# Attention and two feed-forward blocks on one core: all engines and the transfers keep the order of the source

## The chip, the cores and the metric

The kernel runs on one core of a Trainium2 chip. The core's engines run side by side, each through its own list of instructions in order: TensorE (PE in the profile, with its weight loads as PEld), VectorE (DVE), ScalarE (ACT), GpSimd (POOL), and SyncE (SP), which here issues all transfers. The transfers run on 16 DMA engines. An engine that comes to an instruction whose input isn't there waits, and what stands behind it on that engine waits too. The metric is the device time of one execution, in microseconds.

## The reference

4 batches of 12 heads of 448 x 64. The scores of all heads are mixed by a 12 x 12 matrix before the softmax, and the weights by another one after it. The output, as 1792 tokens of 768, goes through two feed-forward blocks.

```python
scores = scale * np.matmul(q, k.transpose(0, 1, 3, 2))
scores = np.einsum('bhij,hg->bgij', scores, w_pre)
scores = scores - np.max(scores, axis=-1, keepdims=True)
attn = np.exp(scores)
attn = attn / (np.sum(attn, axis=-1, keepdims=True) + 1e-09)
attn = np.einsum('bhij,hg->bgij', attn, w_post)
x = np.matmul(attn, v)              # then as (1792, 768)
x = (((x @ w1) * (x @ w2)) @ w3) @ w_out
h = x @ w_in
return np.maximum(0.01 * h, h) @ w_out2
```

## The kernel before

**Tiles.** Each batch has its 448 query rows in four chunks of 120, 120, 120 and 88. A chunk has blocks of 10 query rows (12 blocks, in the last chunk 9, of which the last has 8 rows), so a block is 10 rows x 12 heads = 120 partitions. There are 180 blocks in 16 chunks.

**Scores.** `qk` multiplies q and k for a pair of heads. q and k are split before into a high part (ACT, line 77) and the rest (DVE, line 80), by `q_split` (for a chunk, 0.8 and 0.9 us) and `k_split` (for pairs of heads), and three products of the parts are added. ACT copies the result from PSUM to a tile `s` (DVE half of it in the first two chunks), and each four heads go to a DRAM buffer `sdr`. `relayout` reads them back as 120 partitions of (row, head), two blocks at once, into `sr`.

**A block's work.** `premix` mixes the heads by one matmul with `kpre` into a PSUM bank `pm` (two banks); DVE takes the maximum `mx`, ACT the exponential `e` with its sums `sm`; POOL adds 1e-9 to `sm`, DVE takes the reciprocal `rc`, POOL scales `kpost` by it into `kr`. `postmix`, three blocks behind (LAG), multiplies `e` and `kr` into `po`, and DVE copies this into `ap`. When a chunk is complete, `av` multiplies `ap` with v in two halves, DVE copies the result `px` to `y`, and it goes to `scr`.

**Work in between.** Weights of the feed-forward blocks come as 64-bit words: 32 pieces of `w_out` and `w3` are turned into 32-bit ones during the attention: a load to `wr`, an absolute value on ACT (line 96), four steps on DVE (lines 97 to 104), a store. `fold` multiplies them together at the start of the feed-forward part; the load and split of its first operand `wo` (ACT and POOL, line 385) already runs among the last blocks.

**What sets the order.** In the loop over the blocks (n, with t the block's place in its chunk), each pass calls premix of block n, relayout of n + 6 (AHEAD), the qk of the chunk two further on (QAHEAD; two pairs of heads at t = 0, 2 and 4, in the short chunk at 0, 1 and 2), loads and splits, av where due, postmix of n - 3. PE keeps this order (`manual_schedule` with PE alone). For DVE, ACT, POOL and for SP's queue of transfers, a planner with a model of times chooses the order, and so decides how far ahead of its reader a load stands. `issue_after` only keeps some transfers behind a relayout. q of a chunk is loaded at t = 4, split at t = 0 of the next one, ahead of the first qk that reads it:

```python
if ci + QAHEAD < len(order):
    if t % gap == 0 and t // gap < 3:
        if t == 0:
            q_split(*order[ci + QAHEAD])
        for p in (2 * t // gap, 2 * t // gap + 1):
            qk(*order[ci + QAHEAD], p)
if t == 4 and ci + QAHEAD + 1 < len(order):
    q_load(*order[ci + QAHEAD + 1])
```

Of the kernel before, what the change touches and what calls it, by code (L numbers as in the profile page):

```python
# [23 lines left out]
def attention_moe_kernel(ctx: ExitStack, tc, qt, kt, vt, w_pre, w_post, w1, w2, w3t, w_out, w_in2, w_out2, out):  # L24
# [7 lines left out]
    nc = tc.nc  # L32
# [11 lines left out]
    AHEAD, QAHEAD, LAG, START = 6, 2, 3, 20  # L44
# [46 lines left out]
    def convert(pool, t, shape):  # L91

# [4 lines left out]
        nc.vector.tensor_scalar(out=cf, in0=cf, scalar1=F64_TINY, scalar2=F64_HUGE, op0=ALU.max, op1=ALU.min)  # L97
        nc.vector.tensor_scalar(
            out=c, in0=c, scalar1=0x07FFFFFF, scalar2=3, op0=ALU.bitwise_and, op1=ALU.logical_shift_left
        )  # L100
        nc.vector.scalar_tensor_tensor(
            out=c, in0=hi, scalar=0xC0000000, in1=c, op0=ALU.bitwise_and, op1=ALU.bitwise_or
        )
        nc.vector.scalar_tensor_tensor(  # L104
            out=c, in0=lo, scalar=29, in1=c, op0=ALU.logical_shift_right, op1=ALU.bitwise_or
        )
        return cf

    def attention():
        with ExitStack() as es:  # L110
# [8 lines left out]
            es.enter_context(tc.manual_schedule(engines={mybir.EngineType.PE}))  # L119
# [7 lines left out]
            def constants():  # L127
                for n, w in enumerate((w_pre, w_post)):
                    nc.sync.dma_start(out=wrep[:, n, :], in_=w.unsqueeze(0).to_broadcast([IB, H, H]))
                eye = ident[:R, :R].rearrange("p (i h) -> p i h", h=H)  # L130
# [13 lines left out]
            gate, kls, qls, raws = {}, {}, {}, []  # L144
            kst, vst, qst, st = {}, {}, {}, {}
            srt, ets, krs, apt = {}, {}, {}, {}

            def k_load(b, g):

                kls[b, g] = ld.tile([P, 2, S], F32, tag="kl", name="kl", bufs=3)  # L150
                gate["k"] = nc.sync.dma_start(out=kls[b, g], in_=kt[b, :, 2 * g:2 * g + 2, :])

            def k_split(b, g):
                t = kls.pop((b, g))
                for r in range(2):
                    kst[b, 2 * g + r] = kv.tile([P, 2, S], F32R, tag="ks", name="ks", bufs=NPAIR + 2)
                    split(kst[b, 2 * g + r], t[:, r, :])
# [17 lines left out]
            def qk(b, c, p):  # L175
# [17 lines left out]
                if r == HP - 1:  # L193
                    nc.sync.dma_start(out=sdr[b, c][:, 2 * g * HP:2 * (g + 1) * HP, :], in_=st[b, c][:m])

            def relayout(n):

                b, c, t = blocks[n]
                bl = chunks[c][2]
                o, nb = bl[t]  # L200
                if t % 2 == 0:
                    pair = wk.tile([IB * H, 2, S], F32, tag="sr", name="sr", bufs=4)
                    if t + 1 < len(bl) and bl[t + 1][1] == nb:
                        src = sdr[b, c][o:o + 2 * nb].rearrange("(g i) h j -> (i h) g j", g=2)
                        gate["sr"] = nc.sync.dma_start(out=pair[:nb * H], in_=src)
# [6 lines left out]
            def premix(n):  # L212
                b, c, t = blocks[n]
# [13 lines left out]
                )  # L227
                rc = wk.tile([IB * H, 1], F32, tag="rc", name="rc")
                nc.gpsimd.tensor_scalar(out=sm[:r], in0=sm[:r], scalar1=1e-9, scalar2=None, op0=ALU.add)
# [5 lines left out]
                ets[n], krs[n] = e, kr  # L235

            def postmix(n):
                b, c, t = blocks[n]
# [15 lines left out]
                nc.vector.tensor_copy(ap[:, :, :, o:o + nb], po[:, :, :, :nb])  # L254

            def av(b, c, g):
# [18 lines left out]
                if g == 1:  # L275
                    nc.sync.dma_start(out=scr[b][:, :, c0:c0 + ni], in_=y[:, :, :ni])
# [3 lines left out]
            def conv_load(src, dst, r, c0, n):  # L280
                words = src[r * P:(r + 1) * P, 2 * c0:2 * (c0 + n)].unsqueeze(1)
                raws.append((load_raw(ws, words, (1, n), 2), dst, r, c0, n))

            def conv_store():
                t, dst, r, c0, n = raws.pop(0)
                nc.sync.dma_start(out=dst[r * P:(r + 1) * P, c0:c0 + n], in_=convert(ws, t, (1, n))[:, 0, :])

            blocks = [
                (b, c, t) for b in range(B) for c in range(len(chunks)) for t in range(len(chunks[c][2]))
            ]  # L290
            order = [(b, c) for b in range(B) for c in range(len(chunks))]
            first = {}
            for n, (b, c, t) in enumerate(blocks):
                if t == 0:
                    first[b, c] = n
# [6 lines left out]
            for g in range(NPAIR // 2):  # L302
                k_load(0, g)
                if g == 0:
                    constants()
# [281 lines left out]
```

## Time and profile before

| | us |
|---|---|
| median of three runs | 1523.85 |
| lowest, highest | 1516.05, 1526.09 |
| the profiled execution | 1523.08 |
| its span, first to last instruction | 1521.0 |
| mean granted TensorE clock | 0.956 |
| PE busy | 1406.3 (92%) |
| DVE busy | 908.6 (60%) |
| ACT busy | 585.5 (38%) |
| POOL busy | 179.2 (12%) |
| first matmul of `fold` | at 621.84 |

Busy times are of the span. The granted clock is the share of full speed at which the chip lets TensorE run. A wait is written "engine, tile, line <- what it waited for". In the groups, "x176 | 111.0, 631" means 176 instructions, 111.0 us busy, 631 ns for one. In the timeline the columns are start, length (us), engine, line, operation, output and inputs, and in brackets the idle time ahead of it. The lines `L185` (qk), `L218` (premix), `L222` (mx), `L225` (e), `L247` (postmix), `L254` (ap), `L267` (av) carry the attention; L77 and L80 are the two halves of every split.

### The profile page before, as it was taken

How to read it: one execution, taken by the hardware profiler on the slowest of the kernel's cores; microseconds unless marked ns; L12 is line 12 of the kernel's file. 1: busy time of each engine (PE TensorE's matmuls, PEld its weight loads, DVE VectorE, ACT ScalarE, POOL GpSimd, SP SyncE). 2: the span in 40 equal slices, each digit the busy share in tenths (PEclk: the TensorE clock that was granted, in tenths of full speed). 3: DMA queues.
4: the chain of work that ended last, by engine and by line, in shares of the span. 5: the costliest groups of instructions: out<-in, count | busy, mean ns of one | idle time of the engine just before them, and what ended most of it. 6: DMA issues, size and time to landing. Idle time of an engine off the chain costs nothing.

```text
span 1521.0 us, 22114 instructions
## 1 busy us (share of the span) xinstructions
PE 1406.3 (92%) x8520; PEld 1211.5 (80%) x8520; DVE 908.6 (60%) x1580; ACT 585.5 (38%) x1117; POOL 179.2 (12%) x374
## 2 busy tenths in 40 slices
PE   4778888888789889999999999999999999999999
PEld 2556656666566657999999999999999999999998
DVE  3455556556656546546653596696866445866962
ACT  3443444344434443333332264253333323552430
POOL 0222222232223354000000000000000000000000
PEclk7899989898889889999999999999999999999999
DMA  7757687679777874554312243333733132432301
GB/s 233 208 163 193 191 241 213 179 212 256 220 204 224 239 218 125 155 184 130 106 54 90 86 146 104 104 125 94 225 99 103 55 99 96 149 101 97 130 24 73
DMA packets 140116, 226.23 MB, mean 149 GB/s; under 512 B 19244, under 2 KB 117548, under 8 KB 139564
## 3 DMA queue, kind: packets, MB, share of 16 engines
q1 hardware_dynamic: 140012, 224.83, 49.7%
q8 instruction: 67, 1.10, 0.3%
q14 instruction: 37, 0.30, 0.1%
HBM read 164.77 MB, written 60.03 MB: 148 GB/s over the span
## 4 chain that ended last, share of the span: by engine, by line
PE 74%; DMA 15%; ACT 3%; DVE 3%; SPq 2%; issue 2%; POOL 0%; POOLq 0%; ACTq 0%; DVEq 0%
PE pm L455 39%; PE po L522 15%; DMA ql<-in_q_dram 6%; PE pm L218 5%; PE po L247 5%; DMA wr<-in_moe_w_dram 4%; PE pw L393 4%; PE px L267 3%; DMA wr<-in_moe_w_out_dram 3%; PE pq L185 2%; ACT e L225 1%; ACT s L192 1%; DMA wof<-wof 1%; DVE ap L254 1%; DMA kl<-in_k_dram 1%
## 5 line engine op out<-in xcount | busy, mean ns | idle before, releaser
L455 PE MATMUL pm<-x,ws 128*128 128x448 f32 x2304 | 477.7, 368 | 0.0
L455 PEld LDWEIGHTS pm<-x,ws 128*128 128x128 f32 x2304 | 432.4, 188 | 43.3
L247 PEld LDWEIGHTS po<-kr,e 120*112 120x112 f32 (+1 forms) x1440 | 181.8, 189 | 87.8 <-issue 68.4
L522 PE MATMUL po<-ws,g 128*128 128x384 f32 x1344 | 234.3, 334 | 0.0
L522 PEld LDWEIGHTS po<-ws,g 128*128 128x128 f32 x1344 | 233.2, 188 | 0.3
L247 PE MATMUL po<-kr,e 120*112 120x120 f32 (+1 forms) x1440 | 196.2, 283 | 17.8 <-DVE ap L254 12.5
L218 PE MATMUL pm<-sr,kpre 120*120 120x448 f32 x360 | 181.8, 590 | 30.8 <-ACT e L225 27.9
L225 ACT ACTIVATE e<-pm,mx 120x448 f32<-120x448 f32 x180 | 113.5, 631 | 187.0 <-DVE mx L222 118.2
L96 ACT ACTIVATE wc<-wr 128x768 f32<-128x768 f32 (+2 forms) x128 | 105.8, 830 | 154.3 <-DVE ws L80 57.9
L80 DVE TENSOR_TENSOR ws<-wc,ws 128x768 fp32r<-128x768 f32 x96 | 91.5, 955 | 82.1 <-ACT ws L77 80.9
L97 DVE TENSOR_SCALAR wc<-wc 128x768 f32<-128x768 f32 (+2 forms) x128 | 66.1, 517 | 119.6 <-ACT wc L96 119.5
L254 DVE COPY ap<-po 112x480 f32<-112x480 f32 x180 | 117.1, 650 | 31.8 <-PE po L247 25.7
L267 PEld LDWEIGHTS px<-ap,vs 112*64 112x64 f32 x1536 | 90.4, 159 | 46.7 <-ACT s L192 40.3
L222 DVE TENSOR_REDUCE mx<-pm 120x1 f32<-120x448 f32 x180 | 111.7, 621 | 26.4 <-PE pm L218 19.2
L232 POOL TENSOR_SCALAR kr<-kpost,rc 120x120 f32<-120x120 f32 x180 | 116.0, 644 | 96.5 <-DVE rc L230 47.9
L77 ACT ACTIVATE ws<-wc 128x768 fp32r<-128x768 f32 x96 | 80.6, 842 | 118.3 <-PE po L522 73.9
L267 PE MATMUL px<-ap,vs 112*64 112x120 f32 (+1 forms) x1536 | 97.3, 293 | 28.2 <-ACT s L192 20.0
L455 PE MATMUL pm<-h,ws 128*128 128x448 f32 x576 | 119.4, 368 | 0.0
L185 PE MATMUL pq<-ks,qs 64*120 64x448 f32 (+1 forms) x576 | 87.2, 419 | 34.0 <-DVE y L274 12.5
L185 PEld LDWEIGHTS pq<-ks,qs 64*120 64x120 f32 (+1 forms) x576 | 54.9, 191 | 78.4 <-issue 22.2
L455 PEld LDWEIGHTS pm<-h,ws 128*128 128x128 f32 x576 | 108.1, 188 | 10.9
L104 DVE SCALAR_TENSOR_TENSOR wc<-wr,wc 128x768 uint32<-128x768 uint32 (+2 forms) x128 | 111.6, 872 | 1.4
(45 smaller groups left out, 1059.9 us busy)
## 6 DMA issues: line engine op xcount, KB each, us to landing
sr<-sdr SPq DMA_DIRECT2D x88, 420.0 KB
sdr<-s SPq DMA_DIRECT2D x36, 840.0 KB
wr<-in_moe_w_dram SPq DMA_DIRECT2D x32, 768.0 KB
wr<-in_moe_w_in_dram SPq DMA_DIRECT2D x32, 768.0 KB
wr<-in_moe_w_out_dram SPq DMA_DIRECT2D x32, 768.0 KB
wr<-in_moe_w_dram SPq DMA_DIRECT2D x16, 512.0 KB
sdr<-s SPq DMA_DIRECT2D x12, 616.0 KB
wr<-in_moe_w_out_dram SPq DMA_DIRECT2D x16, 384.0 KB
```

Source lines behind the costliest of these rows:

```text
L96: nc.scalar.activation(out=cf, in_=hi.bitcast(F32), func=ACTF.Abs)
L104: nc.vector.scalar_tensor_tensor(out=c, in0=lo, scalar=29, in1=c, op0=ALU.logical_shift_right, op1=ALU.bitwise_or)
L185: nc.tensor.matmul(pq[e][:m], qst[b, c][rows, p, x, :m], kst[b, p][rows, y, :], start=(j == 0), stop=(j == 2))
L218: nc.tensor.matmul(pm[:r], kpre[:r, :nb, :].rearrange("p i h -> p (i h)"), sr[:r], start=True, stop=True)
L222: nc.vector.tensor_reduce(out=mx[:r], in_=pm[:r], axis=AX.X, op=ALU.max, negate=True)
L225: nc.scalar.activation(out=e[:r], in_=pm[:r], func=ACTF.Exp, bias=mx[:r], scale=1.0, accum_out=sm[:r])
L232: nc.gpsimd.tensor_scalar(out=kr[:r], in0=kpost[:r], scalar1=rc[:r], scalar2=None, op0=ALU.mult)
L247: nc.tensor.matmul(po[:, jc, :, :nb], e[:r, jc * JP:(jc + 1) * JP], kr[:r, :, :nb], start=True, stop=True,)
L254: nc.vector.tensor_copy(ap[:, :, :, o:o + nb], po[:, :, :, :nb])
L267: nc.tensor.matmul(px[e * D:(e + 1) * D, p - p0, :ni], vst[b][:, jc, 2 * p + e, :], ap[:, jc, 2 * p + e, :ni], start=(jc == 0), stop=(jc = ...
L455: nc.tensor.matmul(dst, wt[:, a, kk, :], x[:, kk, c, n * S:(n + 1) * S], start=(kk == 0 and j == 0), stop=(kk == kn - 1 and j == 2),)
L522: nc.tensor.matmul(po, g[:, m, a, t * P:(t + 1) * P], wts[m][:, c, 0, cs], start=(m == 0 and j == 0), stop=(m == FQ - 1 and j == 2),)
```

## The change

- `manual_schedule()` now holds for all engines, so within the attention DVE, ACT, POOL and SP run in the order of the source as PE did. `issue_after` goes.
- The source is written as a pipeline of steps. Of block n's work, premix stands first, then the reciprocal and `kr` of block n - 1 (`weigh`), then `sums` of block n, the relayout, qk, av and postmix of n - 3, then loads and splits.
- qk runs at t = 0, 2, 6. q is loaded at t = 4 and split at t = 7, for the chunk after the one whose qk is running; a third q is loaded and split ahead of the loop. k is loaded at t = 1 to 3 of the second chunk of a batch and split one pair of heads at a time, at t = 7 to 11 and at t = 1 of the third.
- Stores of `s`, `y` and converted weights are put in a list and issued at the start of the next step (`flush`).
- The conversion is a generator: in a step that has qk or av (t = 0, 2, 3, 4, 6), from n = 14 on, two of its pieces are issued; three loads are ahead.
- In the other steps, ap of every odd n is copied by ACT and no longer by DVE: 50 of 180.
- At the start all of k is loaded before the small constants, and v after q of the third chunk.

```diff
-    AHEAD, QAHEAD, LAG, START = 6, 2, 3, 20
+    AHEAD, QAHEAD, LAG, START = 6, 2, 3, 14
...
-            es.enter_context(tc.manual_schedule(engines={mybir.EngineType.PE}))
+            es.enter_context(tc.manual_schedule())
...
-                    nc.sync.dma_start(out=sdr[b, c][:, 2 * g * HP:2 * (g + 1) * HP, :], in_=st[b, c][:m])
+                    stores.append((sdr[b, c][:, 2 * g * HP:2 * (g + 1) * HP, :], st[b, c][:m]))
+
+            def flush():
+
+                while stores:
+                    dst, t = stores.pop(0)
+                    nc.sync.dma_start(out=dst, in_=t)
...
-                nc.vector.tensor_copy(ap[:, :, :, o:o + nb], po[:, :, :, :nb])
+                copy(ap[:, :, :, o:o + nb], po[:, :, :, :nb])
...
+                for _ in range(3):
+                    load()
+                yield
+                while raws:
+                    t, dst, n = raws.pop(0)
+                    for cf in convert_steps(ws, t, (1, n)):
+                        yield
+                    stores.append((dst, cf[:, 0, :]))
+                    load()
...
+            QT, AT = (0, 2, 6), (LAG, LAG + 1)
+            filler = conversions()
...
+            q_load(0, 2)
+            v_prep(0)
             for p in range(NPAIR):
                 qk(0, 1, p)
-            with tc.issue_after(gate["sr"].ins):
-                v_prep(0)
-                q_load(0, 2)
+                flush()
+            q_split(0, 2)
             for n in range(NB + LAG):
+                flush()
+                plain = True
                 if n < NB:
-                    b, c, t = blocks[n]
+                    b, c, t, _ = blocks[n]
                     ci = order.index((b, c))
-                    gap = (len(chunks[c][2]) - AHEAD) // 3
+                    plain = t not in QT and t not in AT
                     premix(n)
+                if 0 < n <= NB:
+                    weigh(n - 1)
+                if n < NB:
+                    sums(n)
                     if n + AHEAD < NB:
                         relayout(n + AHEAD)
...
+                    if ci + QAHEAD < len(order) and t in QT:
+                        for r in range(HP):
+                            qk(*order[ci + QAHEAD], HP * QT.index(t) + r)
                 m = n - LAG
                 if m >= 0:
                     tt = blocks[m][2]
                     if tt < 2 and m > tt:
                         av(*blocks[m - tt - 1][:2], tt)
-                    postmix(m)
+                    postmix(m, nc.scalar.copy if plain and n % 2 else nc.vector.tensor_copy)
+                if n < NB:
+                    if t == 4 and ci + QAHEAD + 1 < len(order):
+                        q_load(*order[ci + QAHEAD + 1])
+                    if t == 7 and ci + QAHEAD + 1 < len(order):
+                        q_split(*order[ci + QAHEAD + 1])
...
+                        if c == NC - 3 and 1 <= t < 4:
+                            k_load(b + 1, t - 1)
+                        if c == NC - 3 and t >= 7:
+                            k_split(b + 1, t - 7)
+                        if c == NC - 2 and t == 1:
+                            k_split(b + 1, 5)
+                    if n >= START and not plain:
+                        for _ in range(2):
+                            next(filler, None)
```

How the order moves is seen at three places. The first is ACT before the change, where the last scores of the third batch's first chunk are made: the copies of a qk (`s`), the absolute value of a weight piece (`wc`), an exponential, the split of q, and the copies of the next qk.

```order
L192 ACTIVATE s<-pq 120x448 x4
L96 ACTIVATE wc<-wr 128x384
L225 ACTIVATE e,sm<-pm,mx 120x448
L77 ACTIVATE qs<-ql 128x6x120
L225 ACTIVATE e,sm<-pm,mx 120x448
L192 ACTIVATE s<-pq 120x448 x4
```

So three instructions stand between the absolute value and the copies of the next qk. The loads of this `wr` and this `ql` stand on SP, among a store of converted weights (`wof`), a store of scores (`sdr`), a relayout (`sr`) and a store of the output (`scr`):

```order
L286 DMA wof<-wc 128x384
L88 DMA wr<-in_moe_w_out_dram 128x768
L194 DMA sdr_0_65<-s 120x1792
L205 DMA sr<-sdr_2_63 120x2x448
L165 DMA ql<-in_q_dram 128x720
L194 DMA sdr_0_65<-s 120x1792
L276 DMA scr_74<-y 768x1x120
```

One store and one relayout lie between the two loads. With the change, the split of the same q stands on ACT in a plain step, behind the last qk of the chunk before it and ahead of a copy of `ap`:

```order
L200 ACTIVATE s<-pq 120x448 x4
L101 ACTIVATE wc<-wr 128x384
L239 ACTIVATE e,sm<-pm,mx 120x448
L77 ACTIVATE qs<-ql 128x6x120
L239 ACTIVATE e,sm<-pm,mx 120x448
L276 COPY ap<-po 112x48x10
```

It is followed by an exponential and the copy, no longer by the qk that reads it. On SP this q is loaded ahead of the last store of the chunk before it:

```order
L219 DMA sr<-sdr_2_63 120x2x448
L173 DMA ql<-in_q_dram 128x720
L208 DMA scr_74<-y 768x1x120
L219 DMA sr<-sdr_3_64 120x2x448
L88 DMA wr<-in_moe_w_dram 128x1024
L208 DMA sdr_0_65<-s 120x1792
L208 DMA wof<-wc 128x384
```

The load now stands two steps ahead of that last store, and three steps ahead of the split.

The second place is DVE and ACT in the plain steps of a batch's second chunk, where q and k are split. ACT now has, between the exponentials (`e`), the splits (`qs`, `ks`) and a copy of `ap`:

```order
L239 ACTIVATE e,sm<-pm,mx 120x448
L77 ACTIVATE qs<-ql 128x6x120
L77 ACTIVATE ks<-kl 128x448
L239 ACTIVATE e,sm<-pm,mx 120x448
L276 COPY ap<-po 112x48x10
L77 ACTIVATE ks<-kl 128x448
L239 ACTIVATE e,sm<-pm,mx 120x448
```

A split stands between any two exponentials. Before, ACT had the k splits in pairs, among the copies of `s`:

```order
L225 ACTIVATE e,sm<-pm,mx 120x448
L77 ACTIVATE ks<-kl 128x448
L192 ACTIVATE s<-pq 88x448
L77 ACTIVATE ks<-kl 128x448
L192 ACTIVATE s<-pq 88x448
L225 ACTIVATE e,sm<-pm,mx 120x448
```

There two splits stood between two exponentials, with copies that need PE's results; now the splits are spread over six steps, and on DVE the other half of each stands ahead of the next maximum.

The third place is SP's queue at the start. Before, with three relayouts first, then a store of scores, v and q of the third chunk:

```order
L205 DMA sr<-sdr_0_57 120x2x448 x3
L194 DMA sdr_1_58<-s 120x1792
L161 DMA vs<-in_v_dram 112x3072
L165 DMA ql<-in_q_dram 128x720
L205 DMA sr<-sdr_0_57 120x2x448
```

There v and a store go ahead of q. Now:

```order
L219 DMA sr<-sdr_0_57 120x2x448 x3
L173 DMA ql<-in_q_dram 128x720
L169 DMA vs<-in_v_dram 112x3072
L208 DMA sdr_1_58<-s 120x1792 x3
L219 DMA sr<-sdr_0_57 120x2x448
```

q has moved ahead of v and of the stores, which still follow v.

More of the change, by code (lines that the diff above doesn't have):

```diff
@@ L227, in premix, with sums, weigh @@
                 )
+                ets[n], sms[n] = e, sm
+            def sums(n):
+                sm = sms[n][:blocks[n][3]]
+                nc.gpsimd.tensor_scalar(out=sm, in0=sm, scalar1=1e-9, scalar2=None, op0=ALU.add)
+            def weigh(n):
+                r = blocks[n][3]
+                sm = sms.pop(n)
                 rc = wk.tile([IB * H, 1], F32, tag="rc", name="rc")
-                nc.gpsimd.tensor_scalar(out=sm[:r], in0=sm[:r], scalar1=1e-9, scalar2=None, op0=ALU.add)
                 nc.vector.reciprocal(out=rc[:r], in_=sm[:r])
@@ L275, in av, with conversions, load @@
                 if g == 1:
-                    nc.sync.dma_start(out=scr[b][:, :, c0:c0 + ni], in_=y[:, :, :ni])
+                    stores.append((scr[b][:, :, c0:c0 + ni], y[:, :, :ni]))
             ys = {}
[L280 to L286, printed above, removed]
+            def conversions():
+                units = [(w_out, wof, r, c0, DM // 2) for r in range(DF // P) for c0 in (0, DM // 2)]
+                units += [(w3t, w3f, r, c0, DF // 2) for r in range(DF // P) for c0 in (0, DF // 2)]
+                raws = []
+                def load():
+                    if units:
+                        w, dst, r, c0, n = units.pop(0)
+                        words = w[r * P:(r + 1) * P, 2 * c0:2 * (c0 + n)].unsqueeze(1)
+                        raws.append((load_raw(ws, words, (1, n), 3), dst[r * P:(r + 1) * P, c0:c0 + n], n))
+                for _ in range(3):
[7 more added lines that the diff above has]
+                    load()
@@ L288, in attention @@
             blocks = [
-                (b, c, t) for b in range(B) for c in range(len(chunks)) for t in range(len(chunks[c][2]))
+                (b, c, t, chunks[c][2][t][1] * H)
+                for b in range(B) for c in range(len(chunks)) for t in range(len(chunks[c][2]))
             ]
             order = [(b, c) for b in range(B) for c in range(len(chunks))]
[L292 to L295, printed above, removed]
@@ L296, in attention @@
             NB = len(blocks)
-            units = [(w_out, wof, r, c0, DM // 2) for r in range(DF // P) for c0 in (0, DM // 2)]
-            units += [(w3t, w3f, r, c0, DF // 2) for r in range(DF // P) for c0 in (0, DF // 2)]
-            every = (NB - 8 - START) // len(units)
+            NC = len(chunks)
+            QT, AT = (0, 2, 6), (LAG, LAG + 1)
+            filler = conversions()
             q_load(0, 0)
@@ L316, in attention @@
             q_split(0, 1)
+            constants()
+            for n in range(AHEAD):
+                relayout(n)
+            q_load(0, 2)
+            v_prep(0)
             for p in range(NPAIR):
                 qk(0, 1, p)
-            with tc.issue_after(gate["sr"].ins):
-                v_prep(0)
-                q_load(0, 2)
+                flush()
+            q_split(0, 2)
             for n in range(NB + LAG):
+                flush()
+                plain = True
                 if n < NB:
-                    b, c, t = blocks[n]
+                    b, c, t, _ = blocks[n]
```

77 lines of the change are left out of this document (33 added, 44 removed).

## The prediction

> **What bounds the kernel now.** I read the stretches first, cut where the trace shows a new stage, because the page's shares are means over an attention part and a feed-forward part with different limits. The last row is the feed-forward part, from the first matmul of `fold` to the end.
>
> ```profile
> span 1521.0 us, 22114 instructions
> ...
> 26.17:60.16 33.99, 16.38 (x74) 8.94 (x75) 6.71 (x15) 10.45 (x24) 4.07 (x10) 0.70 0.81 244
> 60.16:551.00 490.84, 415.94 (x3202) 303.76 (x3203) 284.79 (x631) 209.39 (x516) 138.40 (x297) 0.90 0.75 210
> 551.00:576.00 25.00, 18.92 (x95) 12.16 (x95) 10.76 (x24) 11.72 (x24) 20.07 (x22) 0.80 0.89 236
> 576.00:621.84 45.84, 44.67 (x479) 35.88 (x473) 29.12 (x63) 15.88 (x39) 15.97 (x39) 1.00 0.35 92
> 621.84:1521.00 899.16, 895.29 (x4610) 840.12 (x4608) 564.34 (x825) 326.08 (x493) 0.00 (x0) 1.00 0.35 110
> ```
>
> The columns are the stretch, its length, the busy time of PE, PEld, DVE, ACT and POOL, the granted clock, the DMA share and GB/s. From 621.84 us on, PE is busy 895.29 of 899.16 us at full clock, and the change doesn't touch that code: it stays. The main loop of the attention, 60.16 to 551, is different. PE is busy 415.94 of 490.84 us at a granted clock of 0.90, so the work in it is 415.94 x 0.90 = 374.3 us of a full-clock PE, and 116.5 us are lost: 74.9 to idleness and 41.6 to the halved clock that follows idleness. No other engine is near its limit (DVE 284.79, DMA 0.75). So the loop is bound by waits, and the next views are the waits (engine, what it waited for, us, times, longest) and one of them in order of time.
>
> ```profile
> ACT qs L77 <- DMA ql<-in_q_dram: 51.9, 13, 9.0
> ACT wc L96 <- DMA wr<-in_moe_w_dram: 44.2, 14, 8.3
> ACT wc L96 <- DMA wr<-in_moe_w_out_dram: 35.0, 14, 5.4
> ...
> PE pm L218 <- ACT e L225: 27.9, 18, 4.3
> ...
> 274.42 2.41 SPq L88 DMA_DIRECT2D wr<-in_moe_w_out_dram  x1
> 277.90 1.96 SPq L165 DMA_DIRECT2D ql<-in_q_dram  x1
> 281.78 0.54 ACT L96 ACTIVATE wc<-wr 128x384 f32<-128x384 f32 x1 [5.40 <-DMA wr<-in_moe_w_out_dram]
> 286.65 0.80 ACT L77 ACTIVATE qs<-ql 128x720 fp32r<-128x720 f32 x1 [3.72 <-DMA ql<-in_q_dram]
> ...
> 284.00:288.00 4.00, 1.47 (x5) 0.79 (x5) 2.60 (x5) 1.35 (x4) 0.37 (x1) 0.50 0.28 71
> ```
>
> This is the whole story of the loop. SP issues the load of a weight piece at 274.42 and of the next q at 277.90; ACT stands at the instruction that reads it until 281.78 and 286.65, 7.4 and 8.75 us after the issues, because the order gives a transfer less time than it takes. Behind the waiting instruction on ACT stand the exponentials, behind them the two pm banks, and so PE: it is busy 1.47 us of the four, at half clock. 51.9 + 44.2 + 35.0 = 131.1 us of such waits in 41 places fit the 116.5 us lost.
>
> **The change, part by part.** First the lengths of the steps at full clock, from the starts of one premix and the next: a plain step, one with two qk pairs, one with an av.
>
> ```profile
> 297.80 0.92 PE L218 MATMUL pm<-sr,kpre 120*120 120x448 f32 x2
> 299.38 0.92 PE L218 MATMUL pm<-sr,kpre 120*120 120x448 f32 x2
> ...
> 272.24 0.92 PE L218 MATMUL pm<-sr,kpre 120*120 120x448 f32 x2
> 275.41 0.92 PE L218 MATMUL pm<-sr,kpre 120*120 120x448 f32 x2
> ...
> 603.15 0.92 PE L218 MATMUL pm<-sr,kpre 120*120 120x448 f32 x2
> 607.52 0.92 PE L218 MATMUL pm<-sr,kpre 120*120 120x448 f32 x2
> ...
> 448.00:496.00 48.00, 44.17 (x336) 31.12 (x334) 31.71 (x70) 22.48 (x56) 16.70 (x34) 1.00 0.81 230
> ```
>
> That is 1.58, 3.17 and 4.37 us.
>
> *Loads ahead of their readers.* q is now loaded at t = 4 and split at t = 7: an av step, a plain one and a qk step lie between (4.37 + 1.58 + 3.17), and the exponential of step 7, so some 10 us against the 8.75 us measured. The weight pieces are loaded three units ahead, a unit takes two of the five steps that are not plain, so over 15 us. Both waits should go. What the DMAs need: 0.75 x 490.84 = 368 us of all 16 engines for this stretch. At the share of 0.89 that the row of 551 shows this takes 413 us, so PE's 374.3 can't be reached, but 413 is a floor below what follows. I leave 6 us for q that comes late (0 where the lead holds, 13 x 3 = 39 where every q is 3 us late).
>
> *What the order of the source costs.* Now DVE and ACT run strictly as written, and the splits are written behind the step's exponential and ahead of the next maximum. The durations:
>
> ```profile
> L225 ACT ACTIVATE e<-pm,mx 120x448 f32<-120x448 f32 x176 | 111.0, 631 | 182.3 <-DVE mx L222 118.2 <-DVE rc L230 61.2 <-POOL sm L229 2.6
> L222 DVE TENSOR_REDUCE mx<-pm 120x1 f32<-120x448 f32 x176 | 109.2, 620 | 25.5 <-PE pm L218 18.6 <-ACT s L192 0.2
> L254 DVE COPY ap<-po 112x480 f32<-112x480 f32 x176 | 114.9, 653 | 30.9 <-PE po L247 24.8
> L192 ACT ACTIVATE s<-pq 120x448 f32<-120x448 f32 x120 | 56.8, 544 | 6.3 <-PE pq L185 6.1
> L77 ACT ACTIVATE qs<-ql 128x720 fp32r<-128x720 f32 x10 | 8.0, 801 | 42.1 <-DMA ql<-in_q_dram 42.1
> L80 DVE TENSOR_TENSOR qs<-ql,qs 128x720 fp32r<-128x720 f32 x10 | 9.0, 905 | 26.1 <-ACT qs L77 26.1
> L77 ACT ACTIVATE ks<-kl 128x448 fp32r<-128x448 f32 x18 | 9.5, 569 | 11.3 <-DMA kl<-in_k_dram 11.3
> L80 DVE TENSOR_TENSOR ks<-kl,ks 128x448 fp32r<-128x448 f32 x18 | 11.0, 624 | 12.0 <-ACT ks L77 12.0
> ```
>
> A q split at t = 7 makes a chain from one maximum to the next: mx 0.62, e 0.63, qs high 0.80, qs low 0.91, in all 2.96 us where a plain step has 1.58; where ACT also copies an ap, 0.54 more. PE waits for an exponential two steps back and so absorbs some 0.7 us, but the qk step ahead leaves DVE about 1 us late (its ap copy waits for po behind the qk, then come two conversion pieces). I take 2.05 us for the nine splits in a chunk of 12 blocks, 0.5 us for the others, whose next step is a qk step: about 20 us. A k split makes 0.62 + 0.63 + 0.57 + 0.62 = 2.44 us, with an ap copy on ACT 2.98; against 1.58 that is 1.13 over on the mean. It stands in t = 7 to 11 of the second chunk and t = 1 of the third, together about 7 us in each of three batches: 21 us. The bounds of these two terms: 0, if DVE and ACT run ahead (the row of 448 to 496 loses only 3.8 of 48 us with such splits in it), and 60, if nothing is absorbed and each handover costs another 0.1 us.
>
> *The clock.* During the k splits PE is busy some 60%. What that does, two neighbouring stretches show:
>
> ```profile
> 552.00:560.00 8.00, 4.88 (x30) 3.35 (x29) 3.97 (x9) 4.51 (x10) 5.55 (x7) 1.00 0.97 244
> 560.00:568.00 8.00, 6.76 (x21) 4.20 (x21) 2.47 (x7) 4.12 (x9) 6.56 (x8) 0.51 0.84 235
> ```
>
> PE at 4.88 of 8 us is followed by eight at 0.51. A relapse costs some 3 us a batch, none costs 0; I take 2 in each of three, 6 us. [...]
>
> *ap on ACT.* 50 of 180 copies move, all in plain steps, where ACT has e 0.63 and little else in 1.58 us. The trace shows no such copy; the nearest rows are 0.54 (448 columns, ACT) and 0.65 (this copy, DVE). Either fits beside PE's work, and DVE is relieved of 50 x 0.65 = 33 us that bound nothing. I price it at nothing beyond the chains above; the low end is a gain of 5 us where DVE was late, the high end 50 x 0.3 = 15 us.
>
> *Av and px behind a late DVE*: 3 us (0.2 us in 15 chunks). Stores a step late, sums and weigh apart: hidden, since `s` is reused a chunk later, relayouts run 6 steps ahead, and kr is due two steps after weigh; if that cover goes, PE waits at po.
>
> *The start.* q of chunk 2 and then q of chunk 3 hold it up.
>
> ```profile
> 22.24 1.31 SPq L205 DMA_DIRECT2D sr<-sdr  x3
> 23.67 0.38 SPq L194 DMA_DIRECT2D sdr<-s  x1
> 24.09 0.39 SPq L161 DMA_DIRECT2D vs<-in_v_dram  x1
> 24.52 0.43 SPq L165 DMA_DIRECT2D ql<-in_q_dram  x1
> ...
> 38.44 0.80 ACT L77 ACTIVATE qs<-ql 128x720 fp32r<-128x720 f32 x1 [9.01 <-DMA ql<-in_q_dram]
> ...
> 49.15 1.03 SPq L165 DMA_DIRECT2D ql<-in_q_dram  x1
> ...
> 58.09 0.64 ACT L77 ACTIVATE qs<-ql 128x528 fp32r<-128x528 f32 x1 [6.39 <-DMA ql<-in_q_dram]
> ```
>
> Ahead of the first q lie three sr (1260 KB), one s store (840 KB) and v (1344 KB), and it lands at 38.44, 16.2 us after the first of them was issued: 3804 KB in 16.2 us. Now only the sr lie ahead, 1620 KB with q itself, so 6.9 us and landing near 29: 9.3 us earlier. But v still lies ahead of the s stores whose buffers that step needs, so ACT copies no earlier than about 38. I count 4.3 us there and, for the second q, which is loaded earlier, the 7.2 us until 60: 11.5 us, between 3 and 16.5.
>
> *The end of the attention* (551 to 576, where `fold` splits its weights on ACT and POOL between the blocks) isn't touched, and its splits stand in bunches as before: 0.
>
> **The sum.** The loop: 374.3 + 20 + 21 + 6 + 3 + 6 = 430.3 us for 490.84, 60.5 less. With the start, 72.0. The profiled execution took 1523.08 us, so 1451.1; the median of the runs is 0.8 higher: 1452.
>
> **The rivals.**
> 1. *The chains don't bite* (a quarter). Then the loop loses what 448 to 496 loses, 8%: 374.3 / 0.92 = 406.8, but the DMAs need 413, so 77.8 less there: 1523.9 - 77.8 - 11.5 = 1435. With a DMA share of 0.95, no loss beyond it (387) and the best start (16.5) it would be 1404. For it: that row. Against it: the k splits are written into consecutive plain steps, where nothing covers them.
> 2. *The waits only move* (0.15). More work per time means longer queues; if q and pieces land in 12 us instead of 8.75, ACT waits again. With half of the 116.5 us left beside the 50 new ones the loop takes 374.3 + 58 + 50 = 482, and the time is 1523.9 - 8.6 - 11.5 = 1504. Against it: the pieces have twice the lead they need.
> 3. *Slower* (0.1): the sr loads come late. SP too runs in written order, so a relayout stands behind the store ahead of it, which waits for ACT's copies. The lead is six steps, at least 5 x 1.58 + 3.17 = 11 us. 92 loads late by 0.9 us each cost 83 us, which eats the gain of 72 and more: 1535. It decides from a landing about 12 us after issue. Against it: 8.75 us measured with full queues.
>
> **How the numbers follow.** My forecast, the chains as priced (1435 to 1485), has 0.5, rival 1 has 0.25, rival 2 0.15, rival 3 0.1. About 1% is what a measurement of this kernel can tell from no change, that is 15 us. Faster by over 1% (below 1509): 0.5 + 0.25 + most of rival 2 (0.13), 0.88. Slower: half of rival 3, 0.05. Within 1%: the rest, 0.07. The range leaves out rival 3, the slow half of rival 2 and the far end of rival 1: 1415 to 1490.
>
> **What would show it.** Right: ACT waits for ql and wr shrink from 131.1 us to under 20; the first PE matmul of `fold` starts near 550 instead of 621.84; the stretches after t = 7 of each chunk show PE idle some 2 us, those of the k splits a step of about 2.7 us. Wrong: ACT still waiting at qs for ql (rival 2), PE pm waiting for DMA sr (rival 3), a DMA share of 0.9 and more through the loop (the DMAs bind), or table loads around the ap copies on ACT.

## The result and the profile after

The changed kernel takes 1445.94 us (median of 4 runs, 1444.09 to 1449.61) against 1522.46 for the kernel before on the same chip (median of 4): a ratio of 0.9505, 95% interval 0.9467 to 0.9543. The prediction was 1452, between 1415 and 1490. The profiled execution after took 1449.61 us, its span is 1447.5. The busy times of the page:

```profile
PE 1378.9 (95%) x8520; PEld 1187.9 (82%) x8520; DVE 872.1 (60%) x1530; ACT 607.3 (42%) x1167; POOL 173.0 (12%) x374
```

Three stretches (length; PE, PEld, DVE, ACT, POOL busy; clock; DMA share; GB/s). The first is of the kernel before, the second of the changed one: both run from the start of the fourth block's postmix to the second `av` of the 13th chunk, a stretch called the main stretch from here on. The third is the part from `fold` on after the change.

```profile
60.19:543.04 482.85, 407.98 (x3119) 297.10 (x3119) 280.57 (x623) 206.71 (x510) 136.78 (x293) 0.90 0.75 210
46.57:469.96 423.39, 381.63 (x3108) 274.80 (x3106) 244.39 (x568) 223.47 (x551) 128.09 (x290) 0.96 0.82 241
548.42:1447.50 899.08, 895.28 (x4610) 840.01 (x4608) 564.16 (x825) 326.83 (x493) 0.00 (x0) 1.00 0.35 110
```

The group of `fold`'s first product, with the starts of its first and last matmul:

```profile
L437 PE MATMUL pw<-wo,ws x384: 334/334/443, 548.4 to 615.3; 128*128 128x384 f32 x192
```

`fold` now starts at 548.42 instead of 621.84 us, 73.4 us earlier, and what follows takes 899.08 us instead of 899.16: the whole gain lies in the attention. In the main stretch PE is idle 41.8 us instead of 74.9, and busy 381.6 us instead of 408.0 for the same work, since the clock is 0.96 instead of 0.90. The waits of ACT and of PE in the attention after its start (us, times, longest) show what went:

```profile
ACT wc L101 <- DMA w3f<-wc: 10.3, 6, 4.8
...
ACT wc L101 <- DMA wof<-wc: 9.1, 5, 2.9
ACT wc L101 <- DMA wr<-in_moe_w_out_dram: 7.1, 1, 7.1
ACT qs L77 <- DMA ql<-in_q_dram: 3.1, 1, 3.1
...
PE pm L232 <- ACT e L239: 28.3, 27, 3.8
...
PE pm L232 <- DMA sr<-sdr: 6.0, 4, 2.2
```

In the main stretch the waits for q and weight pieces were 115.7 us in 39 places before (131.1 in 41 with the start); now they are two waits, 10.2 us together. New is a wait for the store of converted weights (`wof<-wc`, `w3f<-wc`, 19.4 us): the conversion has two buffers, and its stores now go a step late. What still holds PE is the exponential, 28.3 us in 27 places. In order of time nearly all of them lie where splits are (ACT's column of the k splits, DVE's maximum and the low half, PE's premix):

```profile
223.67 0.62 DVE L236 TENSOR_REDUCE mx<-pm 120x1 f32<-120x448 f32 x1
224.38 0.63 ACT L239 ACTIVATE e<-pm,mx 120x448 f32<-120x448 f32 x1 [1.29 <-DVE rc L252]
225.01 0.56 ACT L77 ACTIVATE ks<-kl 128x448 fp32r<-128x448 f32 x1
225.16 1.01 PE L232 MATMUL pm<-sr,kpre 120*120 120x448 f32 x2 [1.11 <-ACT e L239]
225.60 0.63 DVE L80 TENSOR_TENSOR ks<-kl,ks 128x448 fp32r<-128x448 f32 x1 [0.69 <-ACT ks L77]
226.15 0.62 DVE L236 TENSOR_REDUCE mx<-pm 120x1 f32<-120x448 f32 x1
226.86 0.64 ACT L239 ACTIVATE e<-pm,mx 120x448 f32<-120x448 f32 x1 [1.29 <-DVE rc L252]
227.48 0.56 ACT L276 COPY ap<-po 112x480 f32<-112x480 f32 x1
...
229.08 0.62 DVE L236 TENSOR_REDUCE mx<-pm 120x1 f32<-120x448 f32 x1
```

From one maximum to the next it is 2.48 us, and 2.93 us where ACT also copies an `ap`. Each engine waits for the other in turn: maximum, exponential, high half, low half, and only then the next maximum, which had its input long before: the premix for the one at 226.15 started at 222.22 and took 1.01 us.

### The profile page after: what moved, and what is told of

It is laid out like the page before. It is cut to its first block, busy times and chain, and to the rows that moved or that the text cites. A ratio compares the mean times of both kernels' runs of the same rounds, so it can differ in the third digit from the quotient of the medians.

```text
span 1447.5 us, 22193 instructions
## 1 busy us (share of the span) xinstructions
PE 1378.9 (95%) x8520; PEld 1187.9 (82%) x8520; DVE 872.1 (60%) x1530; ACT 607.3 (42%) x1167; POOL 173.0 (12%) x374
## 4 chain that ended last, share of the span: by engine, by line
PE 80%; DMA 6%; ACT 5%; DVE 4%; issue 3%; POOL 1%; SPq 0%; DVEq 0%; ACTq 0%; POOLq 0%
PE pm L499 41%; PE po L566 16%; PE po L269 6%; PE px L289 5%; PE pm L232 5%; PE pw L437 5%; PE pq L193 3%; DMA sr<-sdr 3%; ACT e L239 2%; DVE mx L236 2%; DMA sdr<-s 1%; ACT s L200 1%; DMA ql<-in_q_dram 1%; DMA wof<-wof 1%; ACT ks L77 1%
## 5 line engine op out<-in xcount | busy, mean ns | idle before, releaser
L269 PEld LDWEIGHTS po<-kr,e 120*112 120x112 f32 (+1 forms) x1440 | 172.2, 180 | 67.2 <-issue 49.2
L232 PE MATMUL pm<-sr,kpre 120*120 120x448 f32 x360 | 176.0, 572 | 36.9 <-ACT e L239 28.3
L269 PE MATMUL po<-kr,e 120*112 120x120 f32 (+1 forms) x1440 | 187.4, 274 | 4.5 <-POOL kr L254 3.7
L254 POOL TENSOR_SCALAR kr<-kpost,rc 120x120 f32<-120x120 f32 x180 | 112.3, 624 | 314.2 <-DVE rc L252 232.6
L276 DVE COPY ap<-po 112x480 f32<-112x480 f32 (+1 forms) x130 | 84.1, 647 | 59.3 <-PE po L269 57.3
L108 DVE SCALAR_TENSOR_TENSOR wc<-wr,wc 128x768 uint32<-128x768 uint32 (+2 forms) x128 | 111.6, 873 | 2.5
L112 DVE SCALAR_TENSOR_TENSOR wc<-wr,wc 128x768 uint32<-128x768 uint32 (+2 forms) x128 | 111.0, 867 | 1.0
L289 PEld LDWEIGHTS px<-ap,vs 112*64 112x64 f32 x1536 | 79.6, 144 | 30.3 <-ACT s L200 17.9
L193 PE MATMUL pq<-ks,qs 64*120 64x448 f32 (+1 forms) x576 | 82.6, 420 | 13.8 <-ACT qs L77 6.2
```

The source lines that it names most:

```text
L108: nc.vector.scalar_tensor_tensor(out=c, in0=hi, scalar=0xC0000000, in1=c, op0=ALU.bitwise_and, op1=ALU.bitwise_or)
L112: nc.vector.scalar_tensor_tensor(out=c, in0=lo, scalar=29, in1=c, op0=ALU.logical_shift_right, op1=ALU.bitwise_or)
L193: nc.tensor.matmul(pq[e][:m], qst[b, c][rows, p, x, :m], kst[b, p][rows, y, :], start=(j == 0), stop=(j == 2))
L232: nc.tensor.matmul(pm[:r], kpre[:r, :nb, :].rearrange("p i h -> p (i h)"), sr[:r], start=True, stop=True)
L254: nc.gpsimd.tensor_scalar(out=kr[:r], in0=kpost[:r], scalar1=rc[:r], scalar2=None, op0=ALU.mult)
L269: nc.tensor.matmul(po[:, jc, :, :nb], e[:r, jc * JP:(jc + 1) * JP], kr[:r, :, :nb], start=True, stop=True,)
```

## The experiments

Ratios are against the kernel before, on the same chip; its median was 1518.8 to 1523.4 us in these comparisons, so differences between kernels of different ones are good to some 4 us. "Fold" is the start of `fold`'s first product (621.84 before, 548.42 after).

**Which engines' order counts.** The changed source, with fewer engines bound to the written order; the planner orders the others.

```diff
-            es.enter_context(tc.manual_schedule())
+            es.enter_context(tc.manual_schedule(engines={PE}))                # first
+            es.enter_context(tc.manual_schedule(engines={PE, SP}))            # second
+            es.enter_context(tc.manual_schedule(engines={PE, DVE, ACT, POOL}))  # third
```

> The changed source, but only PE keeps its order; DVE, ACT, POOL and the transfers are ordered by the planner as before. Theory (the gain comes from loads that stand far ahead of their readers on ACT, which the written order sets): the planner puts loads close to their readers again, ACT waits over 80 us for ql and wr, and the time is 1495 to 1530. Rival (the rewritten pipeline itself, with ap shared between DVE and ACT and qk at t = 0, 2, 6, is what helps): 1440 to 1460 whatever sets the order.

Measured: 1458.54 us, ratio 0.9586 (0.9558 to 0.9614), fold at 558.0. The theory fell: no wait for q is left, and none for the pieces of `w_out`. Most of the gain comes without any order by hand but PE's.

> The changed source; PE and the transfers keep its order, the planner orders DVE, ACT and POOL. Theory (transfers early enough are what counts): ACT's waits for ql and wr stay under 40 us and, since the planner may pull splits out of the chain between maximum and exponential, 1425 to 1470. Rival (the written order of DVE and ACT carries the gain, because the planner puts readers where its model thinks that the data has landed): waits over 80 us, 1490 to 1520.

Measured: 1513.18 us, ratio 0.996 (0.9925 to 0.9994), fold at 613.6. The waits for q and pieces stay under 40 us as the theory has it, but the time is the rival's. ACT now waits 113.6 us for stores of converted weights, 34.6 for q and 23.1 for k:

```profile
ACT wc L101 <- DMA w3f<-wc: 58.7, 13, 8.4
ACT wc L101 <- DMA wof<-wc: 54.9, 13, 7.5
ACT qs L77 <- DMA ql<-in_q_dram: 34.6, 13, 10.5
ACT ks L77 <- DMA kl<-in_k_dram: 23.1, 9, 5.1
```

With the transfers fixed and the readers free, the planner puts the readers ahead of where the transfers let them run. The third kernel, where the planner orders the transfers behind readers in written order, doesn't have this loss.

> The changed source; PE, DVE, ACT and POOL keep its order, the planner orders the transfers alone. Theory (transfers early enough are what counts): it depends on where the planner puts the loads of q; if they slip towards their reader, ACT waits 30 us or more for ql and the time is 1460 to 1500. Rival (the order of DVE, ACT and POOL carries the gain): within 10 us of the changed kernel, 1436 to 1456.

Measured: 1446.69 us, ratio 0.9508 (0.9424 to 0.9591). With DVE, ACT and POOL in written order it is 12 us less than 1458.5; that of SP adds nothing that can be told within this interval, which is wide. The main stretches of the first kernel and of the third show two effects that oppose each other:

```profile
71.21:479.79 408.58, 375.03 (x3108) 274.55 (x3106) 242.73 (x540) 220.11 (x541) 129.03 (x290) 0.96 0.80 227
58.32:472.92 414.60, 373.36 (x3108) 269.22 (x3106) 244.33 (x568) 222.32 (x551) 130.79 (x290) 0.98 0.82 233
```

The main stretch of the changed kernel, with all engines in written order, starts at 46.57 and takes 423.39 us. So, against the first kernel, the order by hand earns 25 us at the start and costs 15 us behind it.

**What the lead of q is worth.** The load of q moves from t = 4 to just ahead of its split.

```diff
-                    if t == 4 and ci + QAHEAD + 1 < len(order):
+                    if t == 7 and ci + QAHEAD + 1 < len(order):
                         q_load(*order[ci + QAHEAD + 1])
-                    if t == 7 and ci + QAHEAD + 1 < len(order):
                         q_split(*order[ci + QAHEAD + 1])
```

> The changed kernel with one edit: q is loaded at t = 7, just ahead of its split, no longer at t = 4. Theory: 13 times ACT waits some 7 to 9 us at the split, about 100 us in all, PE loses 5 to 8 us each time with the clock's relapse, and the time is 1446 + 65 to 105 = 1510 to 1550, so that this one lead is worth the whole gain. Rival (q's lead matters little, since PE works on or the DMAs bind anyway): under 1465.

Measured: 1560.34 us, ratio 1.0255 (1.0207 to 1.0302), 114 us more than the changed kernel and slower than before.

```profile
ACT qs L77 <- DMA ql<-in_q_dram: 112.3, 14, 12.6
...
PE pm L232 <- ACT e L239: 106.3, 25, 13.5
```

14 waits of 8.0 us on the mean cost 114 us. Its main stretch:

```profile
49.16:582.41 533.25, 399.28 (x3108) 287.45 (x3106) 244.61 (x568) 225.16 (x551) 123.46 (x290) 0.86 0.66 190
```

PE is idle 134.0 us in it, 92 more than in the changed kernel: most of a wait of ACT at a split reaches PE, through the exponential behind it. Another 18 us are PE's busy time, longer for the same work at a clock of 0.86.

**Where the short lead of before came from.** In the source of before the load of q stands eight steps ahead of its split (t = 4 to t = 0), in the changed one three. So the source can't be why before had 8.75 us between them. What holds the load back there is `issue_after`, which keeps it behind a relayout. First the load of q alone is taken out of it, then all of the loop:

```diff
-                    with tc.issue_after(gate["sr"].ins):
+                    if t == 4 and ci + QAHEAD + 1 < len(order):
+                        q_load(*order[ci + QAHEAD + 1])
+                    with tc.issue_after(gate["sr"].ins):          # first
...
-                    with tc.issue_after(gate["sr"].ins):
+                    if True:                                      # second
```

> The kernel before, with one edit: the load of q in the loop no longer stands under issue_after, so the planner may put it on SP's queue as early as its buffer allows; all else, the pieces of weights too, stays held behind a relayout. In the source of before the load stands eight steps ahead of the split, yet the trace has only 8.75 us between them. Theory (the short lead of before came from issue_after, not from where the source has the load): ACT's waits for ql fall from 51.9 us to under 10, those for wr (79 us) stay, and since they take part of the place, the time falls by 20 to 50 us: 1475 to 1500. Rival 1 (the planner itself puts loads late): ql waits and time stay, 1510 to 1530. Rival 2 (the waits only move): ql waits go, wr waits grow by as much, 1510 to 1530.

Measured: 1508.25 us, ratio 0.9925 (0.9884 to 0.9966). The waits for q go as the theory has it, those for pieces grow by 14.8 us (79.2 to 94.0), and the gain of 11.6 us lies between theory and second rival:

```profile
ACT wc L96 <- DMA wr<-in_moe_w_dram: 48.2, 15, 9.2
ACT wc L96 <- DMA wr<-in_moe_w_out_dram: 45.8, 13, 7.9
ACT qs L77 <- DMA ql<-in_q_dram: 9.2, 1, 9.2
```

> The kernel before, without issue_after in the loop: loads of q, of k, of v and of the pieces of weights, and the stores, may all go ahead of the relayout. The source is else that of before. Theory: ACT's waits for ql and for wr both fall (131.1 us to under 30) and the kernel comes near the one that has the new source with only PE in written order (1458.5): 1450 to 1480. Rival (the rewritten source is needed for it, or transfers issued early crowd out the relayouts): 1495 or more, with PE waiting for sr or ACT for the store of wc.

Measured: 1466.48 us, ratio 0.9634 (0.9585 to 0.9682), fold at 566.4. Of the 76.5 us that the change gains, some 53 come from removing `issue_after` alone, with the source otherwise as before. In the trace a load of q is issued as soon as a split frees a buffer. There are two buffers, so the load at 254.50 is that of the q which is split at 306.03, 51.5 us later:

```profile
252.72 0.81 ACT L77 ACTIVATE qs<-ql 128x720 fp32r<-128x720 f32 x1
...
254.50 0.36 SPq L165 DMA_DIRECT2D ql<-in_q_dram  x1
...
306.03 0.67 ACT L77 ACTIVATE qs<-ql 128x528 fp32r<-128x528 f32 x1
```

The waits for pieces fell less than expected (44.8 us remain, and 10.7 for q), yet PE's waits for the exponential fell from 27.9 to 11.4 us; why these cost PE so little isn't settled. New are 15.7 us in which PE waits for relayouts, the crowding out that the rival names. Its main stretch:

```profile
68.55:485.40 416.85, 376.29 (x3118) 273.98 (x3119) 269.83 (x589) 200.95 (x500) 133.86 (x294) 0.96 0.79 227
```

It takes 416.85 us, 6.5 less than in the changed kernel, but starts 22.0 us later. So there the removal alone gains all that the change gains; what the changed kernel has over this one is its start.

**The chain in the splits.** The low half of each split is written a step later, behind the next step's maximum and reciprocal:

```diff
-                split(kst[b, p], kls[b, p // 2][:, p % 2, :])
+                src = kls[b, p // 2][:, p % 2, :]
+                hi_act(kst[b, p][:, 0], src)
+                lows.append((kst[b, p][:, 1], src, kst[b, p][:, 0]))
...
-                lo_dve(qs[:, :, 1, :m], t[:, :, :m], qs[:, :, 0, :m])
+                lows.append((qs[:, :, 1, :m], t[:, :, :m], qs[:, :, 0, :m]))
...
                     weigh(n - 1)
+                while lows:
+                    lo_dve(*lows.pop(0))
```

> The changed kernel, with the low half of every q and k split (DVE, line 80) written a step later, behind the reciprocal of the next step instead of ahead of its maximum. This cuts the chain maximum, exponential, high half, low half, maximum; the work is the same. What then limits a step with a k split is the sum on one engine: DVE 0.62 + 0.15 + 0.62 and in every other step 0.65, 1.72 us on the mean, where the trace shows 2.48 and 2.93. Theory (the chain is what the split steps lose): 0.9 us in each of 18 k steps and about 1 us in 12 q steps, 25 to 30 us less, 1412 to 1430. Rival (the steps are held by something else, as the exponentials behind the two pm banks): 1438 to 1452.

Measured: 1417.53 us (1413.42 to 1420.59), ratio 0.931 (0.9274 to 0.9347), 28.4 us less than the changed kernel. DVE in the k splits:

```profile
210.67 0.61 DVE L245 TENSOR_REDUCE mx<-pm 120x1 f32<-120x448 f32 x1
...
211.27 0.60 DVE L80 TENSOR_TENSOR ks<-kl,ks 128x448 fp32r<-128x448 f32 x1
211.80 0.65 DVE L285 COPY ap<-po 112x480 f32<-112x480 f32 x1
212.36 0.61 DVE L245 TENSOR_REDUCE mx<-pm 120x1 f32<-120x448 f32 x1
...
213.49 0.61 DVE L245 TENSOR_REDUCE mx<-pm 120x1 f32<-120x448 f32 x1
214.36 0.16 DVE L261 RECIPROCAL rc<-sm 120x1 f32<-120x1 f32 x1 [0.26 <-POOL sm L255]
214.75 0.62 DVE L80 TENSOR_TENSOR ks<-kl,ks 128x448 fp32r<-128x448 f32 x1 [0.23 <-ACT ks L77]
...
215.86 0.61 DVE L245 TENSOR_REDUCE mx<-pm 120x1 f32<-120x448 f32 x1
```

In the first two of these steps DVE goes from one instruction to the next without standing still for the high half: 1.69 us from the maximum at 210.67 to that at 212.36, and 1.13 to the next, where DVE has no `ap` to copy. The third takes 2.37 us, with short waits for `sm` and for a high half. That the mean of the three is 1.73 us, where the theory had 1.72, is luck: the theory added up lengths that overlap in the trace by some 0.08 us each, and had no waits.

**ap on ACT.** All copies back on DVE, in the changed kernel and in the one with the low halves later.

```diff
-                    postmix(m, nc.scalar.copy if plain and n % 2 else nc.vector.tensor_copy)
+                    postmix(m, nc.vector.tensor_copy)
```

> The changed kernel, with every copy of ap on DVE as before. Theory (the copies on ACT bound nothing): 1438 to 1451; a gain of some 3 us is possible, because in the k splits the steps with a copy on ACT take 2.93 us and those without it 2.48. Rival (DVE needs the relief: 0.62 + 0.15 + 0.65 in each plain step of 1.58 us leaves it no room to catch up): 50 x 0.3 to 50 x 0.6 us more, 1460 to 1476.

Measured: 1436.81 us (1431.54 to 1441.94), ratio 0.9427 (0.9387 to 0.9468): 9.1 us less than with copies on ACT, more than the theory's 3. The intervals of the two ratios just meet (0.9468 here, 0.9467 there), so the size is uncertain.

> The kernel with the low halves a step later (1417.5), and every copy of ap on DVE. On the changed kernel that second edit alone gained 9 us. Theory (a copy on ACT costs because it stands in the chain from one maximum to the next, behind the exponential and ahead of the high half; with the chain cut it costs nothing, and DVE, with 0.62 + 0.15 + 0.62 + 0.65 = 2.04 us in a split step, now wants the relief): no gain, up to 5 us slower, 1415 to 1424. Rival (the copies on ACT hold up the exponential in every plain step): 9 us less again, 1404 to 1411.

Measured: 1415.48 us, ratio 0.9304 (0.9268 to 0.934), against 1417.53: no difference that can be told. So a copy on ACT costs where it stands in the chain, and nothing that these runs can tell once the chain is cut.

**The start, and the end.** The fourth q ahead of the loop and v of the first batch behind the stores of scores; and the low halves of `wo` on DVE.

```diff
-            v_prep(0)
             for p in range(NPAIR):
                 qk(0, 1, p)
                 flush()
+                if p == 1:
+                    q_load(0, 3)
...
-                    if t == 4 and ci + QAHEAD + 1 < len(order):
+                    if t == 4 and 0 < ci < len(order) - QAHEAD - 1:
...
-                    if c == 0 and t == 5 and b > 0:
+                    if c == 0 and t == 5:
```

> The kernel with the low halves a step later (1417.5), with the fourth q loaded ahead of the loop, among the scores of the second chunk, instead of at t = 4 of the first, and v of the first batch at t = 5 instead of ahead of the stores of scores. In the changed kernel this q was issued at 44.32 us and landed at 53.40, after ACT had waited for it 3 us and PE had stood still behind it; v stands ahead of the stores for whose buffers ACT's copies waited at 36.79. Theory (the order on the queue is what the start loses): 5 to 10 us less, 1407 to 1413. Rival (the start is bound by volume, since the DMA share is 0.94 to 0.95 from 30 to 50 us; what goes ahead makes something else late): 1414 to 1422.

Measured: 1415.36 us (1410.87 to 1421.02), ratio 0.9312 (0.9278 to 0.9346): no difference that can be told; the theory fell.

```diff
-                    nc.gpsimd.tensor_tensor(out=wo[:, kk, 1], in0=t, in1=wo[:, kk, 0].bitcast(F32), op=ALU.subtract)
+                    nc.vector.tensor_tensor(out=wo[:, kk, 1], in0=t, in1=wo[:, kk, 0].bitcast(F32), op=ALU.subtract)
```

> The kernel with the low halves a step later (1417.5), with the low halves of wo (the first operand of fold) on DVE instead of POOL, where each takes 1.81 us and stands ahead of sm and kr. The planner orders them among the last blocks. Theory (the 9.8 us that the last chunk but one loses come from kr behind those eight): 4 to 8 us less, 1409 to 1414. Rival (it is wof that lands late, 9.2 us of ACT's waits, or DVE that is late instead): 1415 to 1422.

Measured: 1416.68 us, ratio 0.9323 (0.9296 to 0.9349): the same; here too the theory fell.

**All together**, but for the copies of ap and the low halves of `wo`, which stay; with a third buffer for `wc` in the attention, and v of the later batches loaded in the third chunk of the batch before.

```diff
-                    for cf in convert_steps(ws, t, (1, n)):
+                    for cf in convert_steps(ws, t, (1, n), 3):
...
+                    if n == 5:
+                        v_prep(0)
+                    if c == NC - 2 and t == 8 and b + 1 < B:
+                        v_prep(b + 1)
-                    if c == 0 and t == 5:
-                        v_prep(b)
```

> All together: the low halves a step later, the fourth q ahead of the loop, v of the first batch at t = 5, three buffers for the converted weights instead of two, and v of the later batches loaded at t = 8 of the third chunk of the batch before, instead of at t = 5 of the first chunk. With v there, at 277.69 us in the kernel of 1415.4, the relayout behind it on the queue (280.31) reached PE only at 294.24, after an idle time of 3.63 us; the DMA share is 0.93 to 0.97 in the three stretches where v is loaded. Theory (v pushes the relayouts late once a batch): 3 to 4 us in each of three batches, and some 2 us for the buffer, so 1402 to 1409. Rival (these stretches are bound by volume, and v only makes another chunk late): 1411 to 1419.

Measured: 1399.06 us (1398.31 to 1401.93), ratio 0.9195 (0.9171 to 0.9218), fold at 498.0: 46.9 us less than the changed kernel. A stretch of the kernel of 1415.4 in which v was loaded, and then the same one of this kernel, with the one ahead of it, in which v is loaded now:

```profile
270.00:310.00 40.00, 35.67 (x329) 26.02 (x330) 22.64 (x52) 19.54 (x49) 10.53 (x26) 0.96 0.97 287
```

```profile
230.00:270.00 40.00, 39.74 (x324) 28.25 (x324) 27.26 (x64) 25.07 (x63) 15.30 (x34) 1.00 0.97 299
270.00:310.00 40.00, 39.26 (x382) 28.86 (x380) 26.28 (x60) 21.07 (x54) 11.92 (x29) 1.00 0.94 288
```

PE's waits for `sr` fell from 10.2 us in 4 places to 2.4 in one. The gain is more than the theory had. The buffer and v weren't tried apart, but the traces point to v for most of it: with the third buffer ACT's 17.8 us of waits for stores of converted weights are gone, yet PE's waits for the exponential, by which such waits reach it, fell only from 8.5 to 6.2 us.

## Why the prediction was right

The time came 6 us below the forecast; the two profiled executions lie 73.5 us apart, where 72.0 were forecast. That the sum is so close is in part luck: the clock cost more than forecast, and idleness less. Step by step:

- *Where the time is lost.* Right: the part from `fold` on stayed, and the time came out of ACT's waits. That such waits reach PE is shown by the late q: for 112.3 us of waits 114 us, of which 92 are PE's idle time in the main stretch.
- *Loads ahead of their readers.* The waits went as forecast (131.1 us to 17.1 with the start, under 20), and the 6 us left for a late q hold: the second q of the start, 3.1 us of ACT and about 4 of PE. But the cause was put in the wrong place. The prediction took the new places in the source (load at t = 4, split at t = 7) for the new lead; before had a longer lead in its source, and lost it to `issue_after`, which the text ahead of the prediction passes over as one that "only keeps some transfers behind a relayout". Removing that alone gives some 53 us of the 76.5, and in the main stretch 66.0 us where the change gains 59.5.
- *The loop and the start.* Two states that both kernels pass through, before and then after, show the size of the terms: the postmix of the fourth block, and the second `av` of the 13th chunk.

```profile
60.19 1.11 PE L247 MATMUL po<-kr,e 120*112 120x120 f32 x4 [6.35 <-DVE ap L254]
543.04 1.14 PE L267 MATMUL px<-ap,vs 112*64 112x120 f32 x18 [0.65 <-ACT s L192]
```

```profile
46.57 1.07 PE L269 MATMUL po<-kr,e 120*112 120x120 f32 x8
469.96 1.25 PE L289 MATMUL px<-ap,vs 112*64 112x120 f32 x20
```

  The start is 13.6 us earlier (forecast 11.5). From the first state to the second it is 423.4 us instead of 482.9, 59.5 less (forecast 60.5 for the loop up to 551). From there to the second `av` of the 15th chunk, at 604.00 and 530.84, it is 60.9 us instead of 61.0 (forecast: no gain at the end).
- *The chains in the splits.* Right in mechanism and in the size of a step. For k: forecast 2.44 and 2.98 us, measured 2.48 and 2.93. For q: the three steps behind t = 7 of a first or third chunk, from premix to premix, take 6.2 to 7.3 us instead of 4.7, on the mean of six 2.0 more (forecast 2.05). Forecast were 41 us for all of them, of which cutting them gave 28.4 back, a part of it by the clock: PE's busy time of the whole span fell with it from 1378.9 to 1369.1 us for the same 8520 matmuls. DVE's own work, 0.62 + 0.15 + 0.62 and in every other step 0.65 more, stays in these steps. Rival 1, that they don't bite, is out for the changed kernel. The row of 448 to 496, on which it rested, is a weak witness: it has one q split, at 479.82, and no k split.
- *ap on ACT.* Priced at nothing beyond the chains, within -5 to 15. It costs 9.1 us, and nothing measurable once the chain is cut, so it is the 0.54 us that the step of the chain had for it, not a term of its own: the experiments agree with that, though 16 split steps with a copy on ACT give only 7.2 us at the 0.45 us measured. The clock may be the rest: its mean is 0.985 to 0.989 in the four runs with all copies on DVE, and 0.982 to 0.987 in those of the changed kernel.
- *The clock.* Mis-sized. Forecast: a relapse of 2 us a batch. The stretches about the k splits of one batch:

```profile
236.00:240.00 4.00, 1.79 (x11) 0.88 (x11) 3.27 (x9) 2.52 (x7) 1.92 (x3) 1.00 0.93 209
240.00:244.00 4.00, 4.00 (x48) 4.00 (x48) 0.70 (x3) 1.79 (x6) 1.04 (x3) 0.57 0.87 247
```

  And PE's matmuls between them, with the longest gap:

```profile
239.88 4.34 PE L289 MATMUL px<-ap,vs 112*64 112x120 f32 x48 [1.90 <-ACT s L200]
```

  That is 4.00 x 0.43 = 1.7 us. But the other two batches relapse for eight us, and the last kernel shows what the main stretch takes at full clock:

```profile
92.00:100.00 8.00, 7.50 (x24) 4.62 (x26) 4.25 (x10) 4.14 (x12) 2.88 (x7) 0.60 0.43 129
368.00:376.00 8.00, 5.64 (x50) 4.99 (x50) 3.63 (x9) 3.96 (x10) 2.30 (x4) 0.63 0.84 238
```

```profile
44.27:421.24 376.97, 365.42 (x3108) 262.91 (x3107) 245.74 (x568) 220.58 (x551) 131.88 (x290) 1.00 0.90 272
```

  PE is busy 381.6 us in the changed kernel and 365.4 in the last one, so the clock costs 16 us where the forecast had 6. PE's idle time is 41.8 us, 8 less than the 50 of the other terms (20 + 21 + 6 + 3). The two errors nearly cancel.

  PE's idle time just ahead of these slow stretches was 1.90 us (at 239.88), 2.15 (at 92.14) and 2.36 us (at 370.71). How long or how often PE has to be idle before the clock falls, no run shows.
- *Rival 2, the waits only move.* They moved only in part: the 19.4 us for stores of converted weights are the new ones, which the prediction did not name.
- *Rival 3, late relayouts.* Its mechanism is real but small: four waits for `sr`, 6.0 us. Three of them, at 192.51, 321.11 and 455.15, ended 13.8 to 14.5 us after the issue, each behind a load of v, beyond the 12 us that the rival named; in the kernel of 1415.4 one such wait is 3.63 us long.
- *The floor of the transfers* in rival 1, 413 us at a share of 0.89, was mis-sized. For the main stretch the same sum gives 0.75 x 482.85 / 0.89 = 407 us, and the last kernel takes 377.0 at 0.90. What failed is that the engines' time was taken as fixed: it is 0.75 x 482.85 = 362 us before and 0.90 x 376.97 = 339 us here, for 101 and 103 MB.

## What to carry to other kernels

When an in-order engine waits for a transfer, ask what decides when the transfer is issued, before moving its line in the source: here a constraint held it back, and dropping it was worth more than writing the order out: some 53 of the 76.5 us. When an order is written out by hand, look for chains that go from one engine to the other and back within a step; here, moving one half of an operation a step later gave 28 us. And look at the start and the rest apart: the written order won 25 us at the start and lost 15 us to the planner's behind it, until its chains were cut. A big load with time to spare should not stand ahead of a load that is due soon: behind v three relayouts came late, 13.8 to 14.5 us after their issue.

## What the runs showed of the hardware

Landing times spread widely within one kernel. The trace tells the landing of only some of the 16 loads of q (128x720 in twelve, 128x528 in four): five in the kernel without `issue_after`, from 2.8 to 19.2 us, 7.7 in the middle, and seven in the last kernel. The shortest is in both the first load of the program. The first row is the kernel without `issue_after`, the second the last one:

```profile
DMA to landing us min/median/max: 2.8/7.7/19.2
```

```profile
DMA to landing us min/median/max: 3.0/7.2/10.8
```

The middle is 2.8 and 2.4 times the shortest landing, so a lead has to be planned by the landings of the kernel itself.
